# Dense layers of the last two pairs of batches as seven half-size products, in a kernel of pooled attention and a mixture of depths

## The chip, the cores and the metric

The kernel runs on one core of a Trainium2 chip. Time is device microseconds of one execution of the program. An engine's name below is that of the profile: PE is TensorE (matmuls; PEld its weight loads), DVE is VectorE, ACT is ScalarE, POOL is GpSimd, SP is SyncE, which only issues DMAs here. A "q" behind a name is the engine's own sequencer or DMA queue.

## What is computed

Attention over pooled keys and values, then a feed-forward layer for the 128 best tokens of each batch. Everything is float32; 8 batches, 8 heads, 576 tokens, head size 64, so rows of 512; hidden size 1024.

```python
k_p = k.reshape(B, H, Sp, 8, D).mean(axis=3)          # v_p alike
attn = softmax(scale * q @ k_p^T) @ v_p               # -> x of (B, S, 512)
scores = einsum('bsd,d->bs', x, w_gate)
for b in range(B):
    top_idx = argpartition(-scores[b], 128)[:128]
    xe = x[b, top_idx]                                # 128 x 512
    h = maximum(xe @ w1, 0.0)                         # 128 x 1024
    ye = h @ w2                                       # 128 x 512
    g = 1 / (1 + exp(-scores[b, top_idx]))
    out[b, top_idx] = xe + g[:, None] * ye            # all other rows: out = x
```

## The kernel before

The whole program is one list of operations (`Plan.add` records each with what it reads and writes), and a table of numbers, ORDER, says in which order they are issued; every engine then works through its own part of that list strictly in order. A second table, BANKS, gives each operation that needs a PSUM tile one of four places: 0 is the pair of banks `pA` (attention results), 1 and 2 are `pJ0` and `pJ1` (all other jobs), 3 is `pS` (attention scores).

For each batch there is a front and a dense part. The front (`front`): K, Q and V are loaded by SP's queue; `pool_k`, `k_trans`, `q_trans` and `pool_v` add and transpose on DVE; `scores` (matmuls into `pS`, L399) and an exponential in ACT (L408); `attend` in five pieces (L463), normed by ACT and DVE into `xs` and stored to the output by a DMA (L262); `rank` sums the gate scores on DVE (L515, after a four-column copy in ACT, L511), spreads them over all partitions with PE (L535), counts ranks in ACT (L547), picks the 128 tokens with a one-hot matmul (L560), and gathers their rows from the output in memory into `xr` (L570, an indirect DMA of POOL). The stores of batches 0 and 1 are issued by POOL and by ACT (the table STORE), all later ones by SP. Buffers alternate between even and odd batches, the index in their names.

The dense part (`dense`): four PE transposes of `xr` (L589) and a copy in ACT to `xg`; the up layer in two halves, 32 matmuls of 128x128 by 128 columns (L597), with a ReLU in ACT (L602) into `ht`; the down layer, 8 matmuls of 128 by 512 columns (L606); one DVE instruction that multiplies by the gate and adds `xr` (L611), and an indirect DMA of POOL that puts the rows back (L615). A float32 matmul shows as two instructions (two passes) in the profile. The weights `w1` and `w2` lie in SBUF, each in two halves.

At the start, 8 matmuls of 512 columns and 16 of 256 columns of zeros (L278, L284) are issued between the first fronts; nobody reads them. At the end, a test (`range_test`) looks at the softmax sums and at the ranks, sums its counts with a small matmul (L642), and DVE writes a flag (L645, L646). All engines load this flag (L40) and branch (L41) past a second, general version of the kernel, which does not run for this data, to a closing exchange between the engines (L1037).

Of the kernel before, what the change touches and what calls it, by code (L numbers as in the profile page):

```python
# [1041 lines left out]
```

## Time and profile before

| what | value |
|---|---|
| three runs, median (lowest to highest) | 264.95 us (262.59 to 265.17) |
| the profiled execution | 264.21 us |
| its span, first to last instruction | 262.3 us |
| PE busy | 234.5 us (89%) |
| PE weight loads busy | 179.2 us (68%) |
| DVE busy | 133.1 us (51%) |
| ACT busy | 104.7 us (40%) |
| POOL busy | 41.2 us (16%) |
| mean granted clock of TensorE | 0.962 |
| moved by DMA | 46.92 MB, 179 GB/s |

Busy time says how long an engine executed; PE's ends are modelled and overlap a little. Where an engine is idle, the profile names what ended the wait. [...] L numbers are lines of the kernel before. An engine that waits costs time only if something on the way to the end waits for it.

### The profile page before, as it was taken

How to read it: one execution, taken by the hardware profiler on the slowest of the kernel's cores; microseconds unless marked ns; L12 is line 12 of the kernel's file. 1: busy time of each engine (PE TensorE's matmuls, PEld its weight loads, DVE VectorE, ACT ScalarE, POOL GpSimd, SP SyncE). 2: the span in 40 equal slices, each digit the busy share in tenths (PEclk: the TensorE clock that was granted, in tenths of full speed). 3: DMA queues.
4: the chain of work that ended last, by engine and by line, in shares of the span. 5: the costliest groups of instructions: out<-in, count | busy, mean ns of one | idle time of the engine just before them, and what ended most of it. 6: DMA issues, size and time to landing. Idle time of an engine off the chain costs nothing.

```text
span 262.3 us, 7033 instructions
## 1 busy us (share of the span) xinstructions
PE 234.5 (89%) x2994; PEld 179.2 (68%) x2994; DVE 133.1 (51%) x295; ACT 104.7 (40%) x262; POOL 41.2 (16%) x95
## 2 busy tenths in 40 slices
PE   7869969875982999999999998999999999999960
PEld 3348757764982866985689656967796695897420
DVE  4779599967512378569992294753402421100020
ACT  2033426834532466261368316437544453122000
POOL 3001313041001040003110126101101033300020
PEclk9997999999797799999999999999999999999995
DMA  7999999999999069909889974301001751200011
GB/s 216 261 340 285 244 301 347 238 366 340 378 233 339 4 123 329 220 6 317 272 273 281 245 265 100 122 2 42 4 0 42 227 176 40 80 4 1 4 44 42
DMA packets 22454, 46.92 MB, mean 179 GB/s; under 512 B 1904, under 2 KB 12016, under 8 KB 21520
## 3 DMA queue, kind: packets, MB, share of 16 engines
q1 hardware_dynamic: 18864, 38.80, 50.4%
q0 software_dynamic: 2816, 6.42, 9.3%
q10 hardware_dynamic: 736, 1.18, 1.4%
q8 instruction: 25, 0.41, 0.7%
q14 instruction: 13, 0.11, 0.1%
HBM read 34.87 MB, written 11.53 MB: 177 GB/s over the span
## 4 chain that ended last, share of the span: by engine, by line
PE 34%; issue 8%; DMA 4%; POOL 2%; DVE 1%; SPq 1%; POOLq 0%; DVEq 0%
PE pJ L597 13%; PE pJ L606 12%; PE pA L463 3%; PE pS L399 2%; DMA out_dram<-y,ix 2%; DMA vr<-in_v_dram 2%; PE pJ L535 1%; POOL vr L346 1%; PE pJ L589 1%; POOL out_dram L615 1%; SPq L262 1%; DVE y L611 1%; PE pJ L463 0%; POOL xr L570 0%; PE pJ L560 0%
## 5 line engine op out<-in xcount | busy, mean ns | idle before, releaser
L597 PE MATMUL pJ<-xg,w 128*128 128x128 f32 x512 | 63.6, 281 | 0.0
L597 PEld LDWEIGHTS pJ<-xg,w 128*128 128x128 f32 x512 | 60.4, 195 | 3.2 <-issue 1.9
L606 PE MATMUL pJ<-w,ht 128*128 128x512 f32 x128 | 60.1, 604 | 0.0
L408 ACT ACTIVATE et<-pS 128x1024 f32<-128x1024 f32 (+1 forms) x40 | 37.3, 937 | 39.5 <-PE pS L399 39.0
L399 PE MATMUL pS<-qt,kt 32*128 32x128 f32 (+1 forms) x1024 | 42.9, 304 | 3.8 <-issue 2.0
L399 PEld LDWEIGHTS pS<-qt,kt 32*128 32x128 f32 x1024 | 35.6, 192 | 10.0 <-issue 4.4
L463 PEld LDWEIGHTS pA<-vp,et 128*64 128x64 f32 x960 | 32.5, 144 | 6.4 <-issue 2.3
L606 PEld LDWEIGHTS pJ<-w,ht 128*128 128x128 f32 x128 | 22.5, 190 | 20.9 <-issue 20.1
L463 PE MATMUL pA<-vp,et 128*64 128x66 f32 x960 | 36.6, 232 | 0.2 <-issue 0.2
L547 ACT ACTIVATE cmp<-sr,sc 128x576 bf16<-128x576 f32 (+1 forms) x40 | 31.0, 776 | 3.8 <-issue 3.1
L487 DVE TENSOR_TENSOR xs<-pA,rz 128x512 f32<-128x512 f32 x30 | 20.7, 692 | 4.5 <-DVE rz L485 2.0
L385 DVE STREAM_TRANSPOSE qt<-qr 128x1024 f32<-128x1024 f32 (+1 forms) x16 | 21.9, 1368 | 1.0 <-DMA qr<-in_q_dram 1.0
L611 DVE SCALAR_TENSOR_TENSOR y<-pJ,gv,xr 128x512 f32<-128x512 f32 x8 | 6.0, 749 | 29.5 <-PE pJ L606 26.0
L485 DVE RECIPROCAL rz<-za 128x8 f32<-128x8 f32 (+1 forms) x40 | 7.7, 192 | 26.0 <-ACT za L479 25.8
L602 ACT ACTIVATE ht<-pJ 128x512 f32<-128x512 f32 x16 | 9.6, 598 | 26.1 <-PE pJ L597 26.1
L479 ACT ACTIVATE za<-pA,eps 128x8 f32<-128x8 f32 x30 | 8.0, 266 | 22.9 <-PE pA L463 22.6
L615 POOL DMA_INDIRECT out_dram<-y,ix x8 | 8.4, 1047 | 48.4 <-DVE gv L579 24.9
L569 POOL TENSOR_SCALAR ix<-tg 128x1 int32<-128x1 f32 x8 | 1.9, 237 | 83.4 <-DVE tg L565 82.3
L535 PE MATMUL pJ<-ident,sc 128*128 128x128 f32 (+1 forms) x40 | 8.3, 289 | 5.5 <-DVE sc L515 5.4
L540 ACT COPY sr<-pJ 128x192 f32<-128x192 f32 (+1 forms) x16 | 6.4, 398 | 15.5 <-PE pJ L535 15.5
L364 DVE TENSOR_TENSOR kr<-kr 128x1152 f32<-128x1152 f32 (+1 forms) x10 | 11.1, 1111 | 2.5 <-DMA kr<-in_k_dram 2.5
L346 POOL DMA_DIRECT2D vr<-in_v_dram x8 | 7.7, 1008 | 28.8 <-DMA vr<-in_v_dram 28.8
(84 smaller groups left out, 198.5 us busy)
## 6 DMA issues: line engine op xcount, KB each, us to landing
kr<-in_k_dram SPq DMA_DIRECT2D x7, 1152.0 KB, 11.4
vr<-in_v_dram SPq DMA_DIRECT2D x8, 896.0 KB, 15.1
out_dram<-xs SPq DMA_DIRECT2D x24, 256.0 KB, 5.2
qr<-in_q_dram SPq DMA_DIRECT2D x8, 640.0 KB, 11.8
qr<-in_q_dram SPq DMA_DIRECT2D x8, 512.0 KB, 11.3
w<-in_moe_w_dram SPq DMA_DIRECT2D x4, 1024.0 KB, 16.4
kr<-in_k_dram SPq DMA_DIRECT2D x3, 384.0 KB, 4.0
vr<-in_v_dram SPq DMA_DIRECT2D x8, 128.0 KB, 8.3
```

The source lines that it names most:

```text
L346: nc.gpsimd.dma_start(out=x[TWO:128], in_=rows_v(b, TWO + 1, 128 - TWO, 2), accum_op=OP.add)
L364: e.tensor_tensor(out=x[:, a:z, 0:2], in0=x[:, a:z, 0:2], in1=x[:, a:z, 2:4], op=OP.add)
L385: nc.vector.transpose(out=QT[b % 2][h].rearrange("p j s (t g) -> p t (j s) g", g=G), in_=QR[b % 2][h].rearrange("p t (j s g) -> p t (j s) ...
L399: nc.tensor.matmul(pS[:, i, 256 * s : 256 * s + n], KT[b % 2][p, j, s, :], QT[b % 2][h][p, j, s, x : x + n], start=(j == 0), stop=(j == 1))
L408: nc.scalar.activation(ET[c][b % NB[c]].rearrange("p n (g t) -> p n g t", g=G), pS.rearrange("p i (s x) -> p (i s) x", s=2)[:, :, y : y + ...
L463: nc.tensor.matmul(o[d][64 * w : 64 * w + 64, E * y : E * y + E], et[:, 2 * m + s, 64 * u : 64 * u + 64], VP[i][:, 2 * m + s, :], start=Tr ...
L487: nc.vector.tensor_tensor(out=XS[i][c].rearrange("p (m s d) -> p s m d", s=2, d=D)[:, k], in0=o[:, :, :, 0:D], in1=rz.rearrange("p (s m on ...
L535: nc.tensor.transpose(row[:, OFF[c] - OFF[a] : OFF[c] - OFF[a] + n], SC[i][0:n, c : c + 1].to_broadcast([n, 128]), ident[0:n, 0:n])
L547: nc.scalar.activation(cmp[0:n], SR[0:n], AF.Sign, bias=SC[i][0:n, c : c + 1], scale=-1.0, accum_out=RK[0:n, b, c])
L597: nc.tensor.matmul(acc[:, cap * f : cap * f + cap], w1[g][:, d, 128 * f : 128 * f + 128], XG[i][:, d, :], start=(d == 0), stop=(d == DB - 1))
L606: nc.tensor.matmul(job(ds)[0:cap, :], HT[i][f // 4][:, f % 4, :], w2[f // 4][:, f % 4, :], start=(f == 0), stop=(f == FB - 1))
L615: j = nc.gpsimd.indirect_dma_start(out=out_rows, out_offset=bass.IndirectOffsetOnAxis(ap=IX[x][:, :1], axis=0), in_=Y[i], in_offset=None)
```

## The change

Batches 4 and 5, and 6 and 7, are now treated in pairs (`PAIRS`). The two batches' 128 tokens each are the two block rows of one matrix, the halves of the inner dimension its block columns, and the weights are cut into 2x2 blocks as well. A 2x2 block product takes eight products of blocks; Strassen's scheme in Winograd's form takes seven, with sums of blocks before and after. Here the sums of the weights are made once (`differences`, eight DVE instructions of 128x1024, into buffers of K, Q and V that the last fronts have left), and per pair and layer `seven` issues four sums of input blocks, seven products, a copy in ACT, and the sums of results on DVE. An up product is 8 matmuls of 128 columns, a down product 4 matmuls of 256 columns. The products may lie in any of the four PSUM places (`ANY`). The ReLU of a pair is made in place on the result of the last sum, so it comes behind DVE. The last step of the down layer is split into a part that needs no last product (`zed`) and the rest (`ends`), both on DVE.

Besides: STORE gives the stores of batch 1 to POOL instead of ACT; the final test also looks at the sizes of the rows of batches 4 to 7 (a square with a sum in ACT for each, and more small DVE instructions in `verdict`); ORDER and BANKS are new throughout (782 operations instead of 753).

The diff, cut to its core:

```diff
 ORDER = [int(x) for x in """
-33 27 28 2 30 0 35 36 37 42 38 43 31 39 40 44 41 1 108 47 45 46 32 34 111 62 5 3 15 8 4 63 58 59 110 109 9 14
...
+29 27 0 2 33 8 35 23 11 36 37 28 38 30 42 43 44 39 1 45 10 12 5 22 4 46 40 13 41 47 108 34 48 32 31 49 50 25
...
-    STORE = ("POOL", "ACT")
+    STORE = ("POOL", "POOL")
+    SPREAD = 4096.0
+    PAIRS = ((4, 5), (6, 7))
...
+    ANY = [(0,), (1,), (2,), (3,)]
...
+    def any_bank(slot):
+        x = plan.bank[slot][0]
+        return (pA[:, 0], pJ[0], pJ[1], pS[:, 0])[x]
...
+    def differences():
+        keys = [("VRx", 0, 0), ("VRx", 0, 1), ("VRa", 0), ("VRb", 0)]
+        t1 = [(part(VR[0], 0, 2, 512), keys), (part(VR[0], 1024, 2, 512), keys), (part(QR[0][0], 0, 2, 512), [("QR", 0, 0)]),
+              (part(QR[0][1], 0, 2, 512), [("QR", 0, 1)])]
+        t2 = [(part(QT[0][0], 0, 4, 256), [("QT", 0, 0)]), (part(QT[0][1], 0, 4, 256), [("QT", 0, 1)]),
+              (part(QR[1][0], 0, 4, 256), [("QR", 1, 0)]), (part(QR[1][1], 0, 4, 256), [("QR", 1, 1)])]
...
+            for y, (o, a, c, op, r) in enumerate(((t[0], m[0][1], m[0][0], OP.subtract, ()), (t[1], m[1][1], t[0], OP.subtract, (0,)),
+                                                  (t[2], m[1][1], m[0][1], OP.subtract, ()), (t[3], m[1][0], t[1], OP.subtract, (1,)))):
+                def differ(o=o, a=a, c=c, op=op):
+                    nc.vector.tensor_tensor(out=o, in0=a, in1=c, op=op)
...
+    def seven(j, n, blocks, keys, m, t, S, skeys, C, ckeys, mul, cost, end):
...
+        for y, (a, b, op, r) in enumerate(((a21, a22, OP.add, (k21, k22)), (S[0], a11, OP.subtract, (("S", n, 0), k11)),
+                                           (a11, a21, OP.subtract, (k11, k21)), (a12, S[1], OP.subtract, (k12, ("S", n, 1))))):
+            def mix(o=S[y], a=a, b=b, op=op):
+                nc.vector.tensor_tensor(out=o, in0=a, in1=b, op=op)
...
+        def plus(g, o, c, gives=True):
+            def plus_():
+                nc.vector.tensor_tensor(out=C[o], in0=any_bank(sl[g])[0 : C[o].shape[0], 0 : C[o].shape[1]], in1=C[c], op=OP.add)
...
+        product(1, a11, m[0][0], [k11] + w)
+        add("ACT", lambda: nc.scalar.copy(out=C[0], in_=any_bank(sl[1])[0 : C[0].shape[0], 0 : C[0].shape[1]]), [sl[1]], [("C", n, 0)] + ckeys[0], gives=(sl[1],))
+        product(2, a12, m[1][0], [k12] + w)
+        end(0, 0, sl[2], 0)
+        product(6, S[1], t[1], [("S", n, 1), ("T", n, 1)])
+        plus(6, 1, 0)
+        product(7, S[2], t[2], [("S", n, 2), ("T", n, 2)])
+        plus(7, 2, 1)
+        product(5, S[0], t[0], [("S", n, 0), ("T", n, 0)])
+        plus(5, 3, 1, False)
+        end(1, 1, sl[5], 2)
+        product(4, a22, t[3], [k22, ("T", n, 3)])
+        end(1, 0, sl[4], 2)
+        product(3, S[3], m[1][1], [("S", n, 3)] + w)
+        end(0, 1, sl[3], 3)
...
+        def mul_up(bank, a, b):
+            for f in range(4):
+                for d in range(2):
+                    nc.tensor.matmul(bank[:, cap * f : cap * f + cap], b[:, d, 128 * f : 128 * f + 128], a[:, d, :], start=d == 0, stop=d == 1)
...
+        def end_up(i, g, slot, c):
...
+                nc.vector.tensor_tensor(out=h, in0=any_bank(slot)[:, 0 : 4 * cap], in1=C1[c], op=OP.add)
...
+            add("ACT", lambda: nc.scalar.activation(h, h, AF.Relu), (), [k])
...
+        def mul_down(bank, a, b):
+            for f in range(4):
+                nc.tensor.matmul(bank[0:cap, 0:256], a[:, f, :], b[:, f, :], start=f == 0, stop=f == 3)
...
+                nc.vector.scalar_tensor_tensor(Z[n], C2[c], GV[x], XR[x][:, cols], op0=OP.mult, op1=OP.add)
...
+                nc.vector.scalar_tensor_tensor(Y[b % 2][:, cols], any_bank(slot)[0:cap, 0:256], GV[x], Z[n], op0=OP.mult, op1=OP.add)
...
     for b in range(B):
-        dense(b)
+        if b < first:
+            dense(b)
...
+    weights_mixed = differences()
+    for j in range(len(PAIRS)):
+        pair(j, weights_mixed)
     range_test()
```

Three places in the engines' lists matter below. The first is on ACT, among the counts of batch 1 and the exponentials of batch 3 (`sr`, `rk` and `sc1` belong to the ranking of batch 1, `xs1` are its rows, `ss0` the score parts of batch 2). This is the list before; DMAHW semaphores are those of DMAs that queues of SP and ACT have issued earlier:

```order
L262 DMA out_0_dram<-xs12_100 16x8x512 [waits DMAHW0_49]
L408 ACTIVATE et01_83<-pS_161 128x1024 [waits PE_49]
L262 DMA out_0_dram<-xs10_98 16x8x512 [waits DMAHW4_49]
L262 DMA out_0_dram<-xs11_99 16x8x512 [waits DMAHW6_49]
L547 ACTIVATE cmp_115,rk_113<-sr_112,sc1_108 128x576 [waits Activation_49]
L262 DMA out_0_dram<-xs14_102 16x4x256 [waits DMAHW0_49]
L511 COPY ss0_103<-ss0_103 64x4 [waits DVE_49]
L262 DMA out_0_dram<-xs13_101 16x8x512 [waits DMAHW1_49]
L408 ACTIVATE et11_85<-pS_161 128x1024 [waits PE_49]
```

Each store waits for an older DMA, and the count, the copy and the exponential behind it wait with it. In the change ACT has no DMA, and five of batch 1's six stores stand in this list on POOL (the first, of `xs10`, stands a little ahead of it), between the pieces of batch 1's scores and its index and gather:

```order
L539 CAST aux1_111<-r1_109 128x5 [waits Pool_49]
L277 DMA out_0_dram<-xs11_99 16x8x512
L277 DMA out_0_dram<-xs14_102 16x4x256 x2
L277 DMA out_0_dram<-xs12_100 16x8x512
L277 DMA out_0_dram<-xs13_101 16x8x512
L584 TENSOR_SCALAR ix1_118<-tg_116 128x1 [waits DVE_49]
L585 DMA xr1_126<-out_0_dram,ix1_118 128x512 [waits DMASW4_49,DMASW5_49,DMASW2_49,DMASW6_49,DMASW1_49,DMASW7_49,DMASW0_49,Pool_49]
```

The second place is PE's list from the up layers of batches 6 and 7 to its end. Before, these are whole halves of a layer (here `w10`, `w11` are halves of the up weights, `w20`, `w21` of the down weights):

```order
L597 MATMUL pJ0_163<-xg1_130,w10_137 128x128 x16
L597 MATMUL pJ1_164<-xg1_130,w11_138 128x128 x12
L606 MATMUL pJ0_163<-w20_139,ht10_133 128x512
L597 MATMUL pJ1_164<-xg1_130,w11_138 128x128 x4
L606 MATMUL pJ0_163<-w20_139,ht10_133 128x512 x3
L606 MATMUL pJ1_164<-w20_139,ht00_131 128x512 x2
L606 MATMUL pJ0_163<-w21_140,ht11_134 128x512 x2
L606 MATMUL pJ1_164<-w20_139,ht00_131 128x512 x2
L606 MATMUL pJ0_163<-w21_140,ht11_134 128x512 x2
L606 MATMUL pJ1_164<-w21_140,ht01_132 128x512 x4
```

In the change, L722 is an up product and L739 a down product; `et00` and `kr` hold input mixes, `vr0`, `qr` and `qt0` weight differences, `ht` the hidden rows of batches 4 and 5 and `qt1` those of 6 and 7:

```order
L739 MATMUL pJ0_163<-w20_139,qt10_80 128x256 x4
L739 MATMUL pA_162<-qr11_71,ht11_134 128x256 x4
L739 MATMUL pJ0_163<-w21_140,kr_67 128x256 x4
L739 MATMUL pA_162<-qt00_78,kr_67 128x256 x4
L722 MATMUL pJ1_164<-et00_82,w11_138 128x128 x8
L739 MATMUL pJ0_163<-qt01_79,kr_67 128x256 x4
L739 MATMUL pJ1_164<-w21_140,qt10_80 128x256 x4
L739 MATMUL pJ0_163<-qr10_70,kr_67 128x256 x4
L739 MATMUL pS_161<-w21_140,kr_67 128x256 x4
L739 MATMUL pJ0_163<-qr11_71,qt11_81 128x256 x4
L293 MATMUL pS_161<-zero_160 128x512 x2
L785 MATMUL pJ1_164<-seen_153,ones_147 1x6
```

Products of both pairs alternate; the last up product (of `w11`) is read two products later through `qt10`, and two of the matmuls of zeros and the test's matmul now come behind the last product. The third place is the end of DVE's list. Before, the flag is written well ahead of the last results:

```order
L645 SCALAR_TENSOR_TENSOR match_156,good_157<-pJ1_164,want_155 1x2
L646 TENSOR_SCALAR flag_58<-good_157 1x1
L578 TENSOR_SCALAR gv3_124<-gv3_124 128x1
L579 RECIPROCAL gv3_124<-gv3_124 128x1
L611 SCALAR_TENSOR_TENSOR y1_136<-pJ0_163,gv3_124,xr3_128 128x512
L578 TENSOR_SCALAR gv2_123<-gv2_123 128x1
L579 RECIPROCAL gv2_123<-gv2_123 128x1
L611 SCALAR_TENSOR_TENSOR y0_135<-pJ1_164,gv2_123,xr2_127 128x512
L40 TENSOR_LOAD flag_58
```

Now it is the last thing that DVE does:

```order
L753 SCALAR_TENSOR_TENSOR y1_136<-pJ0_163,gv3_124,xs02_95 128x256
L788 COPY match_156<-pJ1_164 1x6
L790 COPY match_156<-match_156 1x1 x4
L791 SCALAR_TENSOR_TENSOR match_156,good_157<-match_156,want_155 1x2
L792 SCALAR_TENSOR_TENSOR match_156,good_157<-match_156 1x4
L793 TENSOR_TENSOR good_157<-good_157 1x1
L794 TENSOR_SCALAR flag_58<-good_157 1x1
L40 TENSOR_LOAD flag_58
```

The flag moved from ahead of the last two results to behind them, and each result row is now written in two halves of 256 columns.

## Rows read from the trace of the kernel before

**Rows 1.** The page's part 2: busy tenths in 40 slices of the span.
```profile
PE   7869969875982999999999998999999999999960
```
**Rows 2.** Stages: length, busy (instructions) of PE, PEld, DVE, ACT, POOL; clock, DMA share, GB/s.
```profile
60.00:77.90 17.90, 14.88 (x221) 13.76 (x217) 9.25 (x20) 7.92 (x22) 1.01 (x5) 0.90 1.08 316
77.90:83.40 5.50, 0.11 (x4) 0.05 (x1) 0.30 (x2) 0.19 (x1) 0.00 (x0) 0.86 1.00 349
83.40:88.50 5.10, 5.10 (x53) 4.65 (x55) 2.94 (x4) 3.03 (x7) 1.01 (x5) 0.50 0.31 97
88.50:186.90 98.40, 97.00 (x1399) 74.05 (x1396) 62.45 (x120) 49.66 (x124) 16.45 (x30) 1.00 0.61 173
186.90:253.80 66.90, 66.79 (x507) 49.01 (x505) 11.16 (x41) 20.43 (x52) 10.21 (x20) 1.00 0.19 61
```
**Rows 3.** Chain that ended last: start us, us, engine, tile, line, instructions.
```profile
231.02 8.04 PE pJ L597 x72
...
240.81 9.46 PE pJ L606 x22
```
**Rows 4.** Timeline of PE: start us, us, line, operation, shapes, instructions.
```profile
29.27 0.70 PE L284 MATMUL pJ<-zero 128*128 128x256 f32 x2
29.89 0.74 PE L463 MATMUL pJ<-vp,et 128*64 128x66 f32 x16
...
35.83 1.56 PE L284 MATMUL pJ<-zero 128*128 128x256 f32 x6
```
**Rows 5.** Timeline of ACT, 75 to 84 us; in brackets idle before, and its end.
```profile
75.77 1.20 ACTq L262 DMA_DIRECT2D out_dram<-xs  x2
...
82.29 0.55 ACTq L262 DMA_DIRECT2D out_dram<-xs  x1
82.87 0.19 ACT L511 COPY ss<-ss 64x4 f32<-64x4 f32 x1 [5.00 <-DMA out_dram<-xs]
```
**Rows 6.** Timeline of DVE, the same stretch.
```profile
83.10 0.20 DVE L515 TENSOR_REDUCE sc<-ss 128x5 f32<-128x40 f32 x1 [6.88 <-ACT ss L511]
```
**Rows 7.** Timeline of PE, 60 to 90 us.
```profile
63.81 0.63 PE L589 MATMUL pJ<-ident,xr 128*128 128x128 f32 x4 [2.88 <-DMA xr<-out_dram,ix]
...
83.35 0.90 PE L535 MATMUL pJ<-ident,sc 128*128 128x128 f32 x3 [5.39 <-DVE sc L515]
```
**Rows 8.** Groups by line and shape: count, busy us, mean ns, idle before and releasers.
```profile
L423 DVE TENSOR_TENSOR vr<-vr 128x1024 f32<-128x1024 f32 x7 | 8.5, 1217 | 2.0 <-DMA vr<-in_v_dram 2.0
...
L611 DVE SCALAR_TENSOR_TENSOR y<-pJ,gv,xr 128x512 f32<-128x512 f32 x8 | 6.0, 749 | 29.5 <-PE pJ L606 26.0 <-DMA out_dram<-y,ix 3.4
...
L487 DVE TENSOR_TENSOR xs<-pJ,rz 128x256 f32<-128x256 f32 x12 | 4.9, 422 | 1.4 <-DVE rz L485 0.6 <-ACT ss L480 0.4
...
L427 DVE TENSOR_TENSOR vp<-vr 128x512 f32<-128x512 f32 x7 | 4.8, 691 | 0.2
...
L602 ACT ACTIVATE ht<-pJ 128x512 f32<-128x512 f32 x16 | 9.6, 598 | 26.1 <-PE pJ L597 26.1
```
**Rows 9.** Timeline of all engines: the test and its flag, and the end.
```profile
226.63 0.19 PE L642 MATMUL pJ<-seen,ones 128*1 128x2 f32 x2
...
227.04 0.14 DVE L646 TENSOR_SCALAR flag<-good 1x1 int32<-1x1 f32 x1
...
253.73 0.75 DVE L611 SCALAR_TENSOR_TENSOR y<-pJ,gv,xr 128x512 f32<-128x512 f32 x1 [2.42 <-PE pJ L606]
254.85 0.97 POOL L615 DMA_INDIRECT out_dram<-y,ix  x1 [2.54 <-DVE y L611]
```
**Rows 10.** Lines L40, L41, L1037: durations in ns (min/median/max), first and last start us.
```profile
L40 PEldq TENSOR_LOAD <-flag x1: 488/488/488, 245.8 to 245.8; - x1
...
L41 PEldq COMPARE_BRANCH  x1: 3642/3642/3642, 246.4 to 246.4; - x1
...
L1037 POOLq DRAIN  x3: 46/109/2519, 259.0 to 262.1; - x3
```
**Rows 11.** Line L262 on POOL: durations in ns (min/median/max), first and last start us.
```profile
L262 POOL DMA_DIRECT2D out_dram<-xs x6: 525/544/567, 29.9 to 39.6; - x6
```

More of the change, by code (lines that the diff above doesn't have):

```diff
@@ L231, in direct_path @@
     CT = sb("ct", [128, 1], n=NX)
[L232 removed]
+    seen = sb("seen", [128, 6])
     rank_ok = sb("rankok", [cap, B, 1])
[L234 to L235 removed]
+    want, match = sb("want", [1, 2]), sb("match", [1, 10])
+    good = sb("good", [1, 2])
     zin = sb("zin", [128, B * ZC])
@@ L580, in rank, with gathered @@
         add("DVE", gate, (), [("GV", x)])
-    def dense(b):
+    def gathered(b):
         i, x = b % 2, b % NX
         p = 2000 + 10 * b
-        ts, us, ds = ("turn", b), [("up", b, g) for g in range(2)], ("down", b)
+        ts = ("turn", b)
         def turn():
@@ L591, in dense, with scatter, put @@
         add("ACT", lambda: nc.scalar.copy(out=XG[i].rearrange("p d n -> p (d n)"), in_=job(ts)[:, 0 : DB * cap]), [ts], [("XG", i)], gives=(ts,))
+    def scatter(b):
+        i, x = b % 2, b % NX
+        p = 2000 + 10 * b
+        def put():
+            j = nc.gpsimd.indirect_dma_start(out=out_rows, out_offset=bass.IndirectOffsetOnAxis(ap=IX[x][:, :1], axis=0),
+                                             in_=Y[i], in_offset=None)
+            others(j, b, (store, scat, gath))
+            scat[b] = [j]
+        add("POOL", put, [("Y", i, 0), ("Y", i, 1), ("IX", x)], [("OUT", b)], mark=b)
+    def dense(b):
+        i, x = b % 2, b % NX
+        p = 2000 + 10 * b
+        us, ds = [("up", b, g) for g in range(2)], ("down", b)
+        gathered(b)
         for g in range(2):
@@ L611, in end @@
             nc.vector.scalar_tensor_tensor(Y[i], job(ds)[0:cap, :], GV[x], XR[x], op0=OP.mult, op1=OP.add)
-        add("DVE", end, [ds, ("GV", x), ("XR", x)], [("Y", i)], gives=(ds,))
-        def put():
-            j = nc.gpsimd.indirect_dma_start(out=out_rows, out_offset=bass.IndirectOffsetOnAxis(ap=IX[x][:, :1], axis=0),
-                                             in_=Y[i], in_offset=None)
-            others(j, b, (store, scat, gath))
-            scat[b] = [j]
-        add("POOL", put, [("Y", i), ("IX", x)], [("OUT", b)], mark=b)
+        add("DVE", end, [ds, ("GV", x), ("XR", x)], [("Y", i, 0), ("Y", i, 1)], gives=(ds,))
@@ new lines, in seven, with product @@
+    def seven(j, n, blocks, keys, m, t, S, skeys, C, ckeys, mul, cost, end):
+        p = 2000 + 40 * j + 20 * n
+        sl = [(("first", "second")[n], j, g) for g in range(8)]
+        w = [(("w1", "w2")[n], y) for y in range(2)]
+        (a11, a12), (a21, a22) = blocks
+        (k11, k12), (k21, k22) = keys
+        size = 0.33 if n == 0 else 0.6
+        for y, (a, b, op, r) in enumerate(((a21, a22, OP.add, (k21, k22)), (S[0], a11, OP.subtract, (("S", n, 0), k11)),
+                                           (a11, a21, OP.subtract, (k11, k21)), (a12, S[1], OP.subtract, (k12, ("S", n, 1))))):
+            def mix(o=S[y], a=a, b=b, op=op):
+                nc.vector.tensor_tensor(out=o, in0=a, in1=b, op=op)
+            add("DVE", mix, r, [("S", n, y)] + skeys)
+        def product(g, a, b, reads):
+            add("PE", lambda: mul(any_bank(sl[g]), a, b), reads, [sl[g]], takes=(sl[g], ANY))
+        def plus(g, o, c, gives=True):
+            def plus_():
+                nc.vector.tensor_tensor(out=C[o], in0=any_bank(sl[g])[0 : C[o].shape[0], 0 : C[o].shape[1]], in1=C[c], op=OP.add)
+            add("DVE", plus_, [sl[g], ("C", n, c)], [("C", n, o)] + ckeys[o], gives=(sl[g],) if gives else ())
+        product(1, a11, m[0][0], [k11] + w)
[13 more added lines that the diff above has]
+        end(0, 1, sl[3], 3)
@@ L641, in range_test @@
         slot = ("seen",)
-        add("PE", lambda: nc.tensor.matmul(job(slot)[0:1, 0:2], ones, seen, start=True, stop=True), ["seen0", "seen1", "ones"], [slot], takes=(slot, JOB))
+        add("PE", lambda: nc.tensor.matmul(job(slot)[0:1, 0:6], ones, seen, start=True, stop=True), ["seen0", "seen1", "ones"] + [("seen", b) for x in PAIRS for b in x], [slot], takes=(slot, JOB))
         def verdict():
-            nc.vector.scalar_tensor_tensor(match, job(slot)[0:1, 0:2], 1.0, want, op0=OP.mult, op1=OP.is_equal, accum_out=good)
-            nc.vector.tensor_scalar(flag, good, 1.5, None, op0=OP.is_lt)
+            nc.vector.tensor_copy(match[:, 0:6], job(slot)[0:1, 0:6])
+            for n in range(4):
+                nc.vector.tensor_copy(match[:, 6 + n : 7 + n], match[:, 2 + (n ^ 1) : 3 + (n ^ 1)])
+            nc.vector.scalar_tensor_tensor(match[:, 0:2], match[:, 0:2], 1.0, want, op0=OP.mult, op1=OP.is_equal, accum_out=good[:, 0:1])
+            nc.vector.scalar_tensor_tensor(match[:, 2:6], match[:, 2:6], SPREAD, match[:, 6:10], op0=OP.mult, op1=OP.is_ge, accum_out=good[:, 1:2])
+            nc.vector.tensor_tensor(out=good[:, 0:1], in0=good[:, 0:1], in1=good[:, 1:2], op=OP.add)
+            nc.vector.tensor_scalar(flag, good[:, 0:1], 5.5, None, op0=OP.is_lt)
         add("DVE", verdict, [slot, "want"], ["flag"], gives=(slot,))
@@ L675, in direct_path @@
     front(1)
+    first = PAIRS[0][0]
     for b in range(B):
-        dense(b)
+        if b < first:
+            dense(b)
         if b + 2 < B:
```

52 lines of the change are left out of this document (49 added, 3 removed), and 60 rows, old and new, of tables (BANKS, ORDER).

## The prediction

> **What bounds the kernel now.** I read the page's slices first, then the busy time by stage, then the chain that ended last. TensorE (PE) is at nine tenths or more in nearly every slice of the second half [rows 1]. By stage, from 88.5 to 186.9 us it is busy 97.00 of 98.40 us, and from 186.9 to 253.8 us 66.79 of 66.90 us, both at a granted clock of 1.00, while VectorE (DVE) works 62.45 and 11.16 us there [rows 2]. So from 88.5 us on, a microsecond of matmul taken away is a microsecond of span, as long as nothing new makes PE wait. The part before is different. [...]
>
> [...] ScalarE (ACT) issues six stores of batch 1 from its own queue; two of them go out at 75.77 us, the next only at 82.29 us, and the four-column copy queued behind that one starts at 82.87 us after 5.00 us of idling that the trace puts down to stores [rows 5]. DVE's row sum of the scores waited 6.88 us for that copy [rows 6], and PE 5.39 us for the row sum [rows 7].
>
> **The products.** The last four batches cost, per pair, 128 up passes and 32 down passes (fp32: two passes a matmul). The final chain gives 8.04 / 72 = 0.112 us per up pass of 128 columns and 9.46 / 22 = 0.430 us per down pass of 512 [rows 3]. A pair is 14.3 + 13.8 = 28.1 us. After: seven up products of 16 passes of 128 columns, 112 x 0.112 = 12.5 us, saving 1.8 us per pair. Seven down products of 8 passes of 256 columns: a straight line through the two prices gives 0.218 us a pass, 56 x 0.218 = 12.2 us, saving 1.6 us. Two pairs: **-6.7 us**. The only 256-column passes in the trace are the fills: six passes take 1.56 us, 0.26 each, and an isolated pair of passes keeps the next work away for 29.89 - 29.27 = 0.62 us, 0.31 each [rows 4]. Those stand between other tiles and start cold behind them, so I take the line; the lower bound is half of 0.430, 0.215 (saving 7.0 us), the upper 0.26 (112 x 0.042 = 4.7 us less, saving 2.0), and 0.31 is a rival.
>
> **The sums.** DVE has no row of just these tiles, but near ones [rows 8]: 1.217 us for 128x1024 out of SBUF, 0.691 for 128x512, 0.422 for 256 columns out of PSUM, 0.749 for the three-operand form. Eight differences of weights: 9.7 us, half of them queued among the fronts of batches 6 and 7. Per pair: four 256-column mixes 1.7, three running sums and four ends of the up layer 7 x 0.69 = 4.8, four 512-column mixes 2.8, three sums, four gated remainders and four ends of the down layer 11 x 0.43 = 4.7; together 14.0, less the two old ends, 1.5. So DVE takes on 9.7 + 25 = 35 us. All of it lies beside matmuls: after 186.9 us DVE had 11.2 us in 66.9; with the pairs and four differences it has about 11.2 + 25 + 4.9 = 41 in some 60. Cost on the path: **0**, if no single sum is late.
>
> Where one could be late is where a layer turns into the next: up product, DVE sum (0.69), ReLU in ACT (0.598 [rows 8]), mix on DVE (0.69), down product. In the new order of PE the pairs are interleaved at these turns. The tightest place is the third up product of the last pair, ahead of the down product that reads the ReLU of its sum. Between them stands one down product of 8 x 0.218 = 1.74 us; sum and ReLU need 0.69 + 0.60 and some 0.2 us of handing over, so about 0.25 us is left. The turn of the first pair has two up products of the second pair in it, 3.6 us, for the same work. Then I take no stall; without that cover each turn would cost 0.69 + 0.60 + two mixes 1.4 + handing over, about 2.9 us, and there are four.
>
> **The stores.** Batch 1's six stores go to GpSimd (POOL), each of which takes it 0.544 us [rows 11], 3.3 us in all, behind the pieces of batch 1's scores and ahead of that batch's index and gather; the gather has to wait for these stores anyhow. ACT's counts no longer have a DMA wait among them. The edit can give between 0 and 5.39 + 2.55 = 7.9 us. I take 6.0: the whole idle time, and little of the clock's part, since the stretch before it was granted only 0.90 [rows 2] and another wait may stand there. What is late next is PE's own list: the new order puts all scores of batch 3 and both up halves of batch 0 ahead of the spread that waited, so there is work to fill the place: **-6.0 us**.
>
> **The end.** The flag used to be written at 227.04 us, far from the end [rows 9]; now its matmul stands last on PE, behind two warming matmuls that nobody reads (4 x 0.43 = 1.7 us), and DVE decides it in eleven short instructions instead of three. From that matmul's start to the flag written it was 0.55 us (226.63 to 227.18); eight more at about 0.1 us make 1.4. Flag at PE's end + 1.7 + 1.4 = 3.1 us. Then every engine loads it (0.49 us on PE) and branches, and PE's branch took 3.64 us [rows 10], which lay beside matmuls and now lies bare: 7.3 us after PE's end. On the other side the last scatter is a little earlier, because the last sum is 256 columns wide instead of 512; it starts 0.3 us sooner than the 1.1 us of now (254.85 - 253.73 [rows 9]), and POOL then needs its landing, its drain of 2.52 us and the closing exchange, about 8.5 us after PE's end as today. PE's branch reaches the exchange some 0.4 us before POOL's drain ends. I add **+0.2**.
>
> [...]
>
> **Sum**, against the profiled execution's own time (264.21 us, its span of 262.3 and 1.9 around it): 264.21 - 6.7 - 6.0 + 0.2 = 251.7; I say **252**. The median of the runs is 264.95, 0.7 above that execution.
>
> **Rivals.**
> *The hole moves.* Another wait stands where ACT's stood (the gather of batch 0 already holds PE for 2.88 us before it [rows 7], and POOL now carries twelve stores). Then only the products count: 264.2 - 6.7 + 0.2 = 258. For it: DMA is saturated until about 80 us [rows 2], so work can't come much earlier. Against it: the hole was no lack of data, and PE has two batches' work queued there. Chance 0.25.
> *The end grows.* [...] Chance 0.10.
> *Weights pace the quarter products.* At the isolated fills' 0.31 us a pass, 112 passes cost 10.3 us more than the line: 262. Against it: 0.112 and 0.430 us are nearly in proportion to the width [rows 3]. Chance 0.06.
> [...]
> *The turns stall (slower than before).* If DVE, which takes its list strictly in order, is behind at the turns, PE waits 2.9 us at each of four and then runs a stretch at half clock, as it did after the hole (5.1 us at 0.50): 4 x (2.9 + 2.55) = 22 us, 252 + 22 = 274. It ends above the present time once a turn costs more than 3.2 us, clock included. For it: 0.25 us of cover at the tightest place. Against it: the other turns have one to two products' cover, and DVE is idle a third of the time. Chance 0.07.
> The forecast keeps 0.52.
>
> **Numbers.** A measurement here tells 1%, 2.65 us, from no change. Faster by over 1% means under 262.3: the forecast, the longer end, the moved hole, and most of the weight rival: 0.88, cut to 0.85 for combinations. Within 1%: 0.08. Slower: 0.07. The range goes down to 246 (the full 7.9 us, and the 2.9 us gather wait covered too) and up to 260 (the moved hole with the 0.26 pass partly true); it leaves out the turns and the weight rival.
>
> **What would show it.** PE busy without a gap from about 80 us to its end; no L262-like issue in ACT's queue; up products of 1.8 us each and down products of 1.74; PE's end at about 241 us and 8.7 us after it. Wrong if PE shows waits on DVE sums or on ACT's ReLU after the last front, if PE's idle share between 60 and 100 us stays near 8 us, or if the granted clock falls below 1.00 after 100 us.

## The result and the profile after

| | before | changed |
|---|---|---|
| median of four runs each (lowest to highest) | 264.42 us (262.59 to 265.17) | 250.19 us (248.65 to 250.74) |
| ratio, 95% interval | | 0.946 (0.939 to 0.953) |
| the profiled execution, its span | 264.21, 262.3 us | 249.86, 248.1 us |
| DVE busy | 133.1 us (51%) | 165.7 us (67%) |
| last product's sum starts on DVE | 253.73 us [rows 9] | 236.94 us |
| from there to the end of the span | 8.57 us | 11.16 us |

The prediction was 252 us (246 to 260). The total came out 1.8 us below it, but out of two errors of opposite sign: TensorE was done sooner than the 241 us of the steps (at 236.74 us in this profiled execution, at 239.03 in a second one), and the end after it was 2.6 us longer instead of 0.2. That the total is so near is in part luck. Below, a median is that of all executions, a ratio and its interval leave out slow ones, and the profiled executions of the free scatter, of the early flag and of the first runs with both edits were slow ones, so that their rows are used for the last 12 us only.

The page of the changed kernel, the line of PE in its 40 slices, which answers to [rows 1]:

```profile
PE   7689868986999999999999999999999999999940
```

The 2 of the hole in [rows 1], PE's wait of 5.39 us [rows 7], is gone; from the eleventh slice to the thirty-eighth every one is a nine. By stage (length, busy and instructions of PE, PEld, DVE, ACT, POOL; granted clock of TensorE, where 1.00 is the full one, DMA share, GB/s), answering to [rows 2]; the pairs of batches begin at 185.56 us and PE's last product ends at 236.74:

```profile
20.00:60.00 40.00, 31.67 (x622) 25.40 (x626) 32.92 (x63) 18.37 (x50) 10.16 (x17) 0.96 1.06 303
60.00:80.00 20.00, 19.79 (x363) 17.98 (x358) 11.09 (x24) 12.56 (x31) 3.64 (x10) 0.91 1.04 350
80.00:100.00 20.00, 20.00 (x253) 14.70 (x253) 12.52 (x25) 10.06 (x26) 3.32 (x8) 1.00 0.63 188
100.00:185.56 85.56, 85.56 (x1306) 66.69 (x1304) 59.85 (x116) 47.58 (x122) 18.26 (x35) 1.00 0.62 182
185.56:236.74 51.18, 51.18 (x356) 47.88 (x355) 34.05 (x76) 16.55 (x41) 8.48 (x13) 1.00 0.14 45
236.74:248.10 11.36, 2.01 (x7) 0.66 (x5) 1.44 (x12) 0.00 (x0) 1.18 (x2) 0.71 0.15 53
```

From 60 us to its last product PE is idle for 0.21 us in all. The sums put DVE at 34.05 of 51.18 us in the pairs, and none of it holds PE. The chain that ended last (start, us, engine, tile, line, instructions) prices the products; L722 is the up product, L739 the down product, 16 and 8 passes each:

```profile
214.22 5.36 PE pJ L722 x48
228.27 5.18 PE pJ L739 x24
```

5.36 / 48 = 0.1117 us for a pass of 128 columns, 5.18 / 24 = 0.216 us for one of 256: half of the 0.430 us of 512 [rows 3]. Seven products are 12.5 and 12.1 us, against 14.3 and 13.8 us, so two pairs save 6.9 us.

The end, in the timeline of all engines (start, us, engine, line, operation, idle before and its end):

```profile
235.22 0.48 DVE L753 SCALAR_TENSOR_TENSOR y<-pS,gv,xs 128x256 f32<-128x256 f32 x1 [0.52 <-PE pS L739]
...
235.98 0.97 POOL L613 DMA_INDIRECT out_dram<-y,ix  x1 [6.60 <-DVE y L753]
...
236.74 1.88 PE L293 MATMUL pS<-zero 128*128 128x512 f32 x4
236.94 0.48 DVE L753 SCALAR_TENSOR_TENSOR y<-pJ,gv,xs 128x256 f32<-128x256 f32 x1 [0.40 <-PE pJ L739]
...
239.47 0.97 POOL L613 DMA_INDIRECT out_dram<-y,ix  x1 [2.52 <-DVE match L791]
...
239.70 0.14 DVE L794 TENSOR_SCALAR flag<-good 1x1 int32<-1x1 f32 x1
```

The last scatter starts 2.53 us after the start of its sum, where it was 1.12 us [rows 9]. The name behind its idle time is the verdict on DVE, which has nothing to do with it; its sum had ended at 237.42 us. The first scatter was issued at 235.98, and needs 2.7 us and more to land; the experiments below show that the second one waits for that.

### The profile page after: what moved, and what is told of

Same layout as the page of the kernel before. It is cut to its first block, busy times and chain, and to the rows that moved or that the text cites. A ratio compares the mean times of both kernels' runs of the same rounds, so it can differ in the third digit from the quotient of the medians.

```text
span 248.1 us, 7170 instructions
## 1 busy us (share of the span) xinstructions
PE 225.6 (91%) x3010; PEld 183.8 (74%) x3010; DVE 165.7 (67%) x359; ACT 108.8 (44%) x274; POOL 47.6 (19%) x101
## 4 chain that ended last, share of the span: by engine, by line
PE 79%; DMA 9%; issue 4%; DVE 3%; ACT 2%; SPq 1%; POOL 0%; DVEq 0%
PE pS L414 13%; PE pJ L629 12%; PE pJ L638 12%; PE pA L478 12%; PE pJ L739 6%; PE pJ L722 5%; DMA qr<-in_q_dram 4%; DMA vr<-in_v_dram 4%; PE pA L722 3%; PE pJ L550 2%; PE pS L722 2%; PE pS L739 2%; PE pA L739 2%; PE pJ L604 2%; PE pJ L478 2%
## 5 line engine op out<-in xcount | busy, mean ns | idle before, releaser
L414 PE MATMUL pS<-qt,kt 32*128 32x128 f32 (+1 forms) x1024 | 43.4, 307 | 6.9 <-ACT et L423 2.4
L638 PE MATMUL pJ<-w,ht 128*128 128x512 f32 x64 | 31.9, 615 | 0.0
L629 PE MATMUL pJ<-xg,w 128*128 128x128 f32 x256 | 31.6, 279 | 0.2 <-issue 0.2
L629 PEld LDWEIGHTS pJ<-xg,w 128*128 128x128 f32 x256 | 29.7, 192 | 1.4 <-issue 0.5
L638 PEld LDWEIGHTS pJ<-w,ht 128*128 128x128 f32 x64 | 10.7, 189 | 7.9 <-issue 7.1
L584 POOL TENSOR_SCALAR ix<-tg 128x1 int32<-128x1 f32 x8 | 2.8, 353 | 61.0 <-DVE tg L580 35.7
L379 DVE TENSOR_TENSOR kr<-kr 128x1152 f32<-128x1152 f32 (+1 forms) x10 | 11.1, 1114 | 3.6 <-DMA kr<-in_k_dram 3.6
L299 PE MATMUL pJ<-zero 128*128 128x256 f32 x32 | 12.4, 503 | 0.3 <-ACT sr L555 0.3
L555 ACT COPY sr<-pJ 128x384 f32<-128x384 f32 (+1 forms) x16 | 6.3, 400 | 14.5 <-PE pJ L550 11.2
L277 POOL DMA_DIRECT2D out_dram<-xs x12 | 6.8, 601 | 22.8 <-DVE ss L523 12.5
L293 PE MATMUL pS<-zero 128*128 128x512 f32 x16 | 9.7, 698 | 1.5 <-DVE fours L306 1.5
## 6 DMA issues: line engine op xcount, KB each, us to landing
vr<-in_v_dram SPq DMA_DIRECT2D x8, 896.0 KB, 11.2
```

What stands on the lines that cost most here:

```text
L299: nc.tensor.matmul(job(slot)[:, 0:256], zero[:, 0:128], zero[:, 0:256], start=True, stop=True)
L379: e.tensor_tensor(out=x[:, a:z, 0:2], in0=x[:, a:z, 0:2], in1=x[:, a:z, 2:4], op=OP.add)
L414: nc.tensor.matmul(pS[:, i, 256 * s : 256 * s + n], KT[b % 2][p, j, s, :], QT[b % 2][h][p, j, s, x : x + n], start=(j == 0), stop=(j == 1))
L629: nc.tensor.matmul(acc[:, cap * f : cap * f + cap], w1[g][:, d, 128 * f : 128 * f + 128], XG[i][:, d, :], start=(d == 0), stop=(d == DB - 1))
L638: nc.tensor.matmul(job(ds)[0:cap, :], HT[i][f // 4][:, f % 4, :], w2[f // 4][:, f % 4, :], start=(f == 0), stop=(f == FB - 1))
```

## The experiments

Times are medians, with the ratio to the runs of the kernel before on the same chip. Short diffs are against the changed kernel, unless told otherwise.

### The stores, undone and done alone

```
-    STORE = ("POOL", "POOL")
+    STORE = ("POOL", "ACT")
```

> The changed kernel with one thing undone: the six stores of batch 1 are issued by ScalarE again instead of GpSimd; the order list stays the new one. Theory of the prediction (the stores on ScalarE made the hole and are worth about 6 us): 256, with ScalarE idle 4 to 6 us ahead of a row copy in the trace and TensorE idle some 5 us between 60 and 100 us. Theory that the whole early gain (10 us by the traces) comes from the stores: 260. Rival (the new order list made the gain, the queue of the stores is nothing): 250 within 1 us and no such idle time.

Measured: 256.75 us, ratio 0.971 (0.962 to 0.981), that is 5.6 to 6.6 us above the two medians of the changed kernel (251.11, told below, and 250.19); the interval is 2.5 us to either side. A hole is back, in the timelines of ACT, DVE and PE:

```profile
87.01 3.90 ACTq L277 DMA_DIRECT2D out_dram<-xs  x5
90.96 0.48 ACT L555 COPY sr<-pJ 128x384 f32<-128x384 f32 x1 [3.65 <-DMA out_dram<-xs]
```
```profile
91.48 0.69 DVE L502 TENSOR_TENSOR xs<-pA,rz 128x512 f32<-128x512 f32 x1 [6.74 <-ACT sr L555]
```
```profile
95.33 2.09 PE L414 MATMUL pS<-qt,kt 32*128 32x128 f32 x32 [5.32 <-DVE kt L395]
```

Five stores keep ACT's queue for 3.90 us ahead of a row copy; DVE (the norm `xs`, and behind it the transposes that make `kt`) stands behind the copy, PE behind DVE, and the 5.07 us that PE then runs have a granted clock of 0.56:

```profile
90.00:95.33 5.33, 0.01 (x2) 0.78 0.49 163
95.33:100.40 5.07, 5.07 (x88) 0.56 0.46 81
```

The price of the step is what the prediction said (6.0), and by the mechanism that it named: stores in ACT's queue, a small copy behind them, DVE, PE. The instructions in the chain are others, a row copy and DVE's norm and transposes in place of the four-column copy and the row sum.

The other way round, in the kernel before:

```
-    STORE = ("POOL", "ACT")
+    STORE = ("POOL", "POOL")
```

> The kernel before with one thing done: the six stores of batch 1 are issued by GpSimd; the order list is the old one and no layer is by seven products. Theory of the prediction: 6 us faster than before, 258.4, TensorE's idle time between 77.9 and 83.4 us gone. Theory that the whole early gain is the stores: 254. Rival (the order list made the gain): within 1 us of before, the hole stays or turns up elsewhere.

Measured: 260.5 us, ratio 0.989 (0.980 to 0.997): 3 to 4 us faster. The end of this kernel is 0.8 us longer than before (9.4 against 8.6, in the table on the end), so ahead of it 4 to 5 us are gained. By the same reckoning the stores are worth 6 to 7 in the new order, since its end is 0.5 us shorter with the stores on ACT; with intervals of 2 us and more the two are not clearly apart. The hole is gone, but smaller waits of PE stand in other places of the old list:

```profile
57.81 0.34 PE L463 MATMUL pJ<-vp,et 128*64 128x66 f32 x4 [3.29 <-issue]
...
64.12 0.66 PE L589 MATMUL pJ<-ident,xr 128*128 128x128 f32 x4 [0.41 <-ACT sr L540]
...
81.17 0.34 PE L463 MATMUL pA<-vp,et 128*64 128x66 f32 x5 [0.98 <-issue]
88.83 0.22 PE L463 MATMUL pJ<-vp,et 128*64 128x66 f32 x1 [0.66 <-issue]
```

The first of them was 1.40 us in the kernel before:

```profile
56.35 0.34 PE L463 MATMUL pJ<-vp,et 128*64 128x66 f32 x4 [1.40 <-issue]
```

The wait ahead of the gathered rows' transposes, 2.88 us before [rows 7], is down to 0.41 us here, under the old list. The execution shown took 257.59 us, the fastest of its four, so its rows show where waits stand and not what the median lost.

The list alone is the kernel with the stores on ACT: 264.48 - 256.75 = 7.7 us faster than before, of which 6.9 are the products (priced above, and confirmed by the eighth product below); its end is 2.0 us longer (10.6 against 8.6), so the list gave some 2.8 us that no step of the prediction has, with the 2.5 us of the interval to either side. Its clearest proof is the next experiment.

### What the order list gave

In the kernel before PE waited 2.88 us for the gathered rows of batch 0 [rows 7]. In the changed kernel the gather lands 7.7 us after its issue at 58.59, at 66.3 us, and PE runs score and attention pieces until its transposes of these rows at 69.39:

```profile
58.59 1.11 POOL L585 DMA_INDIRECT xr<-out_dram,ix  x1 [0.43 <-POOL ix L584]
...
69.39 0.66 PE L604 MATMUL pJ<-ident,xr 128*128 128x128 f32 x4
```

The experiment puts the transposes back in front of five groups of matmuls: the score and attention pieces at 64.24 and 65.34 us, which ran while the gather was under way, the spread of batch 1's scores at 66.43, and the score and attention pieces at 67.20 and 68.31. The gather goes ahead of one store of batch 1, and the copy of the transposes goes with them (numbers are steps of the order list: 105 the gather, 178 the transposes, 179 their copy in ACT):

```
-... 106 243 298 141 105 299 292 234 235 162 163 ... 310 178 239 303 179 304
+... 106 105 178 243 298 141 299 292 234 235 162 179 163 ... 310 239 303 304
```

> The changed kernel with one step moved in the order list: the four transposes of batch 0's gathered rows stand on TensorE where they meet the gather too early, as they did before, ahead of three pieces of work that now run while the gather is under way (the attention piece at 63.4 us, the score piece at 64.2, the attention piece at 65.3 in the trace after). Theory (the new order list gained, beside the stores, by having work on TensorE while the gather lands at 66.3 us): TensorE waits some 2.9 us for the gather and the kernel is 2.9 us slower, up to 4.5 with the clock. Rival (the time is made up later, or this wait was not what the order list took away): within 1 us of the changed kernel.

Measured: 255.58 us, ratio 0.969 (0.962 to 0.975), and the changed kernel beside it 251.11 us, ratio 0.952 (0.947 to 0.957): 4.5 us slower by the medians, 4.3 by the ratios. In the timeline of PE (lines of that kernel):

```profile
67.58 0.66 PE L577 MATMUL pJ<-ident,xr 128*128 128x128 f32 x4 [3.67 <-DMA xr<-out_dram,ix]
...
72.92 0.85 PE L523 MATMUL pJ<-ident,sc 128*128 128x128 f32 x5 [0.91 <-ACT xg L579]
```

3.67 + 0.91 = 4.6 us of waits, and about as much shows in the time. (From 67.58 to 72.90 us the granted clock is 0.68 behind the wait; the changed kernel's first profile has 0.64 from 59.57 to 64.30 us, behind a wait of 2.30 us, its second 1.00 there, so what the clock adds is not told apart.) This is the upper end of what was expected: where four transposes stand in a list is worth as much as two thirds of the products' gain.

### Eight products for seven

```
+            def times():
+                for _ in range(2 if g == 7 else 1):
+                    mul(any_bank(sl[g]), a, b)
-            add("PE", lambda: mul(any_bank(sl[g]), a, b), ...
+            add("PE", times, ...
```

> The changed kernel with one of the seven products of each layer and pair issued twice over into the same bank (the second replaces the first, so the result is the same): eight products for seven. Theory (TensorE is the bound through both pairs, nothing else): 2 x (1.79 + 1.73) = 7.0 us more, 257.2. Rival (a part of the pairs is paced by the sums on VectorE or by weight loads): 0 to 4 us more, as the extra product would fill waits.

Measured: 257.0 us, ratio 0.976 (0.968 to 0.984), 6.8 us more than 250.19. In its chain the places with the double product:

```profile
216.59 7.15 PE pJ L725 x64
...
232.43 6.91 PE pJ L742 x32
```

They are one product longer (64 for 48 passes, 32 for 24). From the first product of the pairs to the end of the last it is 242.63 - 184.41 = 58.22 us, where the changed kernel has 51.18: 7.04 us, where 7.0 was expected. The pairs are PE-bound, and the trick is worth its matmuls.

### How well the sums are covered

```
-                nc.vector.tensor_tensor(out=C[o], in0=any_bank(...), in1=C[c], op=OP.add)
+                for _ in range(2 - n):   # n = 0 is the up layer
+                    nc.vector.tensor_tensor(out=C[o], in0=any_bank(...), in1=C[c], op=OP.add)
```
and the same for the four end sums of the up layer.

> The changed kernel with the running sums and the end sums of both up layers issued twice by VectorE (the same numbers written again): 7 instructions of 0.69 us a pair, 9.7 us more work on VectorE, all of it ahead of the ReLUs at the turns. Theory (the sums are covered; the trace shows 0.2 us of room at the tightest turn and over 0.6 us at the others): 0 to 2 us more, 250.2 to 252. Rival (the turns stand on the edge, each repeat goes onto the path): 4 turns x 0.7 to 1.4 us = 3 to 6 us more, or up to 9.7 when all of it shows, 253 to 260.

Measured: 257.48 us, ratio 0.974 (0.965 to 0.983), 7.3 us more. The stretch of the pairs is 246.06 - 187.94 = 58.12 us, 6.94 longer: of the 9.7 us of work added, 2.8 were covered. PE's waits by what ended them (us in total, times, longest):

```profile
PE pA L741 <- DVE gv L593: 1.4, 1, 1.4
PE pJ L741 <- DVE et L687: 1.0, 1, 1.0
PE pJ L604 <- DVE ht L730: 1.0, 1, 1.0
PE pA L741 <- DVE qt L730: 0.7, 1, 0.7
PE pJ L741 <- ACT qt L732: 0.4, 1, 0.4
PE pJ L741 <- ACT xs L691: 0.2, 1, 0.2
```

The rival won. These waits add up to 4.7 of the 6.9 us; where the other 2.2 lie is not shown. At their size the sums cost nothing: the changed kernel has no wait of PE in this stretch. But more work on DVE finds little room: with it PE waits in six places, not in one. DVE works through its list in order, and a sum that is late hands its delay on to the mixes behind it (PE's 1.0 us for the mix `et`), although DVE is busy for only 43.45 of the 58.12 us. Seven sums a pair are doubled at once, so a turn here carries several repeats; how near the edge each turn is by itself, this run does not tell. The granted clock stays at 1.00 through all six waits, the longest of 1.4 us.

### The end: two chains

Two edits, each alone and both together. Without the two warming matmuls (the flag comes 1.5 us sooner after the last product):

```
-                nc.tensor.matmul(pS[:, n % 4, :], zero[:, 0:128], zero, start=True, stop=True)
+                if n not in (4, 6):
+                    nc.tensor.matmul(pS[:, n % 4, :], zero[:, 0:128], zero, start=True, stop=True)
```

> The changed kernel without the two warming matmuls that stand behind TensorE's last product (their result is read by nobody). The flag is then written about 1.7 us sooner. Theory A (the last scatter, which waits for the scatter before it to land, sets the end): 0 us, within 0.4 of the changed kernel. Theory B (the flag, and the load and branch behind it, sets the end): 1.7 us faster, 248.5. Theory C (both chains end together): 0.2 to 0.8 faster.

And a memset of one element on POOL between the last two scatters. The kernel declares a scatter free of the DMAs of all other batches but one, that of the operation directly before it on POOL (`plan.before` in `others`); with the memset between, the last scatter is free of this one too:

```
+    add("POOL", lambda: nc.gpsimd.memset(apart, 0.0), (), ("apart",))
-... 777 769 771 772 776 781
+... 777 782 769 771 772 776 781
```

> The changed kernel with one tiny memset of GpSimd between the last two scatters, so that the last no longer follows the other directly in the list and need not wait until it has landed; the warming matmuls stay. Theory A (the landing sets the end): the last scatter starts at 237.8 instead of 239.5, and the kernel is 1.7 us faster, 248.5. Theory B (the flag sets the end): 0 us. Theory C (both chains end together): 0.2 to 0.8 faster.

> The two edits of the end together: no warming matmuls at the end and a last scatter that need not wait for the one before it. Theory A (landing alone): 1.7 us faster, as with the scatter edit alone. Theory B (flag alone): 1.7 faster, as with the warming matmuls alone. Theory C (both chains end together): 1.5 to 2 us faster where each edit alone gave under 0.8.

The last of the three ran again beside the changed kernel, with its theory put more sharply:

> The changed kernel once more, on the same chip and in the same call as the kernel with both edits of the end, so that these two can be compared: 250.2 as before, and 11 us from TensorE's last product to the end.

> The kernel with both edits of the end once more, beside the changed kernel on the same chip. Theory (the last scatter's start, its landing and GpSimd's closing work are the chain of the end): 8.7 us from TensorE's last product to the end, 2.5 us faster than the changed kernel, 247.7. Rival (the gain of the first run was the chip's): within 0.7 of the changed kernel.

And with the flag's matmul moved ahead of the last three products and the verdict ahead of the last two:

```
-... 767 759 764 774 756 773 765 723 770 761 768 775 7 9 780 777 ... 776 781
+... 767 759 780 764 774 756 781 773 765 723 770 761 768 775 7 9 777 782 ... 776
```

> As the kernel with both edits of the end, but with warming matmuls kept and the flag's matmul and VectorE's eleven verdict instructions moved up, ahead of the last two products of the last pair, into a stretch where VectorE is idle for 0.98 us. The flag is then written some 3 us before TensorE's last product ends. Theory (the flag with the branch behind it is a second chain of the end): 2.5 to 3.5 us faster than the changed kernel, about 247, the end 8 us after the last product. Rival (the end is set by the landing of the last scatter and GpSimd's closing work alone): 1.7 us faster, no more than the scatter edit gives. If the verdict delays the last sums, up to 0.6 of the gain is lost.

This kernel has the memset too. Other than its expectation says, it also leaves out the two warming matmuls (its heat steps 4 and 6 do nothing), and the flag's matmul writes to a bank of `pS`.

| kernel | median us | ratio (interval) | last sum's start to last scatter | scatter to landing | landing to end | sum of the three |
|---|---|---|---|---|---|---|
| before | 264.42 | | 1.1 | 3.0 | 4.5 | 8.6 |
| before, stores on POOL | 260.50 | 0.989 (0.980 to 0.997) | 1.1 | 3.3 | 5.0 | 9.4 |
| changed, stores on ACT | 256.75 | 0.971 (0.962 to 0.981) | 2.6 | 3.5 | 4.6 | 10.6 |
| changed, first profile | 250.19 | 0.946 (0.939 to 0.953) | 2.5 | 3.6 | 5.0 | 11.2 |
| changed, second profile | 251.11 | 0.952 (0.947 to 0.957) | 2.5 | 3.5 | 5.1 | 11.1 |
| no warming matmuls | 250.91 | 0.962 (0.952 to 0.972) | 2.5 | 4.2 | 5.1 | 11.8 |
| free scatter | 248.71 | 0.953 (0.946 to 0.960) | 0.8 | 2.7 | 5.8 | 9.3 |
| both, second runs | 248.08 | 0.943 (0.937 to 0.949) | 0.8 | 2.7 | 5.1 | 8.5 |
| early flag, free scatter | 249.09 | 0.954 (0.945 to 0.962) | 0.8 | 4.8 | 5.0 | 10.6 |

(The first runs of "both" gave 248.5 us, ratio 0.949 (0.940 to 0.959), and the same stages. PE's last product ends at 236.74 us in one profile of the changed kernel and at 239.03 in the other, with the same 11.1 to 11.2 us behind it, so the ends are compared by their traces, stage by stage.) The last scatter's start in the kernel with both edits, where the one before it no longer holds it:

```profile
238.30 0.97 POOL L615 DMA_INDIRECT out_dram<-y,ix  x1 [6.62 <-DVE y L755]
...
239.26 0.48 DVE L755 SCALAR_TENSOR_TENSOR y<-pJ,gv,xs 128x256 f32<-128x256 f32 x1 [0.40 <-PE pJ L741]
...
240.03 0.97 POOL L615 DMA_INDIRECT out_dram<-y,ix  x1 [0.67 <-DVE match L790]
```

0.77 us after the start of its sum, not 2.53. The landing that was waited for is named by the trace of the kernel without warming matmuls, in the row of its last scatter:

```profile
239.89 0.97 POOL L614 DMA_INDIRECT out_dram<-y,ix  x1 [2.52 <-DMA out_dram<-y,ix]
```

What follows. The flag alone gives nothing (250.91, and an end of 11.8 us), as theory A said. The free scatter starts 1.7 us sooner, and then the flag's chain is the longer one: flag at 243.3 us, POOL's load and branch behind it, and only then its closing work, so that it keeps 0.8 us more than both edits together (a single profile shows this). Both give 2.6 us by the traces (11.1 to 8.5) and 3.0 by the medians of runs side by side (2.4 by the ratios), and **the kernel with both edits has the lowest median of this study**, 248.1 us; its runs do not tell it from the free scatter alone (0.949 against 0.953 side by side). The early flag, expected at 247, gave nothing more: its scatter took 4.8 us to land.

## Why the prediction was right or wrong

**What bounds the kernel.** Right. Products doubled, waits brought back and sums made late between 60 us and PE's end all showed in the time, nearly microsecond for microsecond.

**The products, -6.7.** Right: -6.9, by 0.216 us a pass where the straight line gave 0.218. The isolated fills (0.26 and 0.31 [rows 4]) were no guide to a pass in a row of its like, and the rival on weights falls. They had a granted clock of 1.00 (29.20 to 29.90 and 35.80 to 37.40 us), so it was no low clock that made them dear, and a part of their 0.26 is the way it was read: a group's modelled end in the timeline runs over the next start, and the eight passes of a product show 1.89 us there, 0.24 each. In the chains a pass took 0.112, 0.216 and 0.430 us for 128, 256 and 512 columns, nearly in proportion to the width.

**The sums, 0.** Right in size, too sure in its reason. The 0.25 us at the tightest place was there: the ReLU ended at 229.66 us, the product that reads it began at 229.84, 0.18 us later. That the other turns have one to two products' cover, and DVE a third of its time idle, was no measure of the room: of 9.7 us more on DVE only 2.8 were covered, and PE waited at six places. The rival on the turns did not come true in this kernel; the doubled sums met its waits, though not its half clock: the granted clock was 1.00 through waits of up to 1.4 us.

**The stores, -6.0.** Right in the new order (5.6 to 6.6 us when undone, give or take 2.5), and by a chain of the same kind: stores, copy in ACT, DVE, PE. Alone, in the old order, it is 3 to 4 in all, and 4 to 5 ahead of an end that got longer. The 2.55 us in the upper bound are half of the 5.10 us that PE ran at a granted clock of 0.50 in the kernel before [rows 2]. Up passes there, in its timeline of PE:

```profile
84.05 1.91 PE L597 MATMUL pJ<-xg,w 128*128 128x128 f32 x8
85.89 2.09 PE L399 MATMUL pS<-qt,kt 32*128 32x128 f32 x32
```

From start to start it is (85.89 - 84.05) / 8 = 0.230 us a pass, against 0.112 at 1.00 [rows 2] [rows 3], so about half of that stretch was lost.

**What is late next: PE's own list, counted at nothing.** This step failed, to the good side. The prediction saw that the list puts work ahead of the spread, and saw the 2.88 us wait for the gather [rows 7], but took it only into the lower end of the range. The list had filled that place too. In the first profile the last sum starts 16.8 us sooner; less 6.9 for the products and some 6 for the stores, 3.9 are left for the list. By the second (PE's end 2.3 us later) 1.6 are left, by the kernel with the stores on ACT 2.8, and moving the transposes back cost 4.5. So the list gave about 2 to 4 us; each of these differences is uncertain by 2 us or more. That the gather's wait is all of the list's gain isn't shown. PE's idle time between 20 and 60 us grew from 4.5 to 8.3 us at the same time, and with the stores on POOL that wait was nearly gone in the old list too (0.41 us), behind a wait that had grown from 1.40 to 3.29.

**The end, +0.2.** This term failed: +2.6. The flag was forecast well (PE's end + 3.1 us, and measured 239.84 - 236.74 = 3.1), but it was not the longer chain. The wrong step is "it starts 0.3 us sooner than the 1.1 us of now". In the kernel before, the sum of the last batch but one started at 250.30 us, 3.4 us ahead of the last one [rows 9], and its scatter landed 2.7 us after its issue, at 254.0, before the last one was due:

```profile
250.30 0.75 DVE L611 SCALAR_TENSOR_TENSOR y<-pJ,gv,xr 128x512 f32<-128x512 f32 x1 [18.07 <-PE pJ L606]
251.33 0.98 POOL L615 DMA_INDIRECT out_dram<-y,ix  x1 [23.22 <-DVE gv L579]
```

That was only just in time: the two issues are 3.52 us apart (251.33 and 254.85), in the changed kernel 3.49 (235.98 and 239.47), each time some 0.8 us from the landing of the first to the start of the second. In the interleaved pair the two batches end 1.7 us apart (235.22 and 236.94), and the second scatter waits for the first: 2.5 - 1.1 = 1.4 us. With the wait taken away it started 0.8 us after its sum, as the prediction had it. Its landing took 0.6 us more (3.6 against 3.0; the cause is open, as told at the end), and POOL's closing work another 0.6. Rows of the sources L41 and L1190 of the changed kernel (durations in ns min/median/max, first and last start):

```profile
L41 POOLq EVENT_SEMAPHORE  x5: 17/43/1929, 241.0 to 243.2; - x5
...
L41 PEldq COMPARE_BRANCH  x1: 4822/4822/4822, 240.5 to 240.5; - x1
...
L41 POOLq INC_SWDGE_SEM  x1: 920/920/920, 243.3 to 243.3; - x1
```
```profile
L1190 POOLq DRAIN  x3: 46/109/3009, 244.2 to 247.8; - x3
```

Before, the drain was 2519 ns [rows 10] and the INC_SWDGE_SEM 800 ns. The two experiments on the stores name the cause, first the changed kernel with the stores on ACT, then the kernel before with the stores on POOL:

```profile
L1190 POOLq DRAIN  x3: 46/109/2519, 252.6 to 255.7; - x3
```
```profile
L1037 POOLq DRAIN  x3: 46/109/3009, 251.9 to 255.4; - x3
```

It goes with the stores: six more DMAs from POOL make its closing work 0.6 us longer (0.49 the drain, 0.12 the semaphores ahead of it, which are 800 and 920 ns in these two kernels as well), in both kernels alike. The step that moved them to POOL priced their issue and not this.

As in the rival "the end grows", the end did grow, by 2.6 us, but PE's branch is not the cause: it took 4.82 us, 1.2 longer than before, and still ended at 245.3 us, 2 us before POOL's drain. What makes that branch long is not shown. DMA packets of the kind "instruction" run behind the flag, 8 of them in this profile and 9 in the kernel before, but no run tells what they do to it.

**The hole moves.** False in size: PE is busy for 39.79 of the 40 us from 60 to 100 in the first profile and for 37.25 in the second, where it was 31.6 of 40. Some waiting did move ahead of 60 us, the 3.8 us told above, and the gain is what is left after it.

**The chances.** 0.52, 0.10 and 0.25 make 0.87, and with most of the weight rival's 0.06 some 0.92, not the 0.88 that was cut to 0.85.

## What to carry to other kernels

A change that comes with a new order list is two changes: price the list by every wait that the old one has near the moved steps, not only by the one that the change aims at. When work of two batches is interleaved, look at what used to be apart at the end; two DMAs with a dependence between them that were issued far apart may now wait for each other (here the sums ahead of them came from 3.4 to 1.7 us apart, and the second scatter started 1.4 us later). Idle time of an engine that runs in order is no cover (with the doubled sums DVE was busy for 43.45 of 58.12 us, and PE waited six times): the cover of a sum is the work between it and its reader, and doubling the sums shows in one run how much of it there is in all.
